# Sums of quarter products kept in a PSUM bank, and a reordered passage between two experts

## The chip, the core and the metric

The kernel runs on one core of a Trainium2 chip. The core has five engines that work side by side and wait for each other by semaphores: TensorE (PE, matrix products, with the load of its stationary operand counted apart as PEld), VectorE (DVE), ScalarE (ACT), GpSimd (POOL) and SyncE (SP, which here starts transfers). Products land in PSUM, whose banks hold 512 float32 values in each of 128 partitions. The metric is the time of one execution on the device, in microseconds (us).

## The reference

A windowed attention is followed by a mixture of experts with one expert per token. Attention works on `q`, `k`, `v` of shape (4, 8, 768, 64); its result is laid out as `x` of shape (3072, 512).

```python
logits = xn @ en.T / tau                   # cosine of token and expert, 8 experts
expert_idx = np.argmax(logits, axis=1)
gate_w = probs[np.arange(N), expert_idx]
for e in range(E):
    mask = expert_idx == e
    h = np.maximum(x[mask] @ w1[e], 0.0)   # 512 -> 1024
    out[mask] = gate_w[mask, None] * (h @ w2[e])   # 1024 -> 512
```

All is float32.

## The kernel before

**Stages.** Attention and routing take the first 190 us or so; the change does not touch them. They end with the first layer (line 670) for a first block of 256 rows of expert 0, whose hidden values are `fhT`. From there the program is straight: the second layer of that block, then the eight experts in turn, each with the rows that are left for it (at most 512).

**Order.** Inside the expert stage the order of instructions on every engine is the order of the program text (`tc.manual_schedule`). Each engine works through its own list in order; an instruction that waits holds all behind it.

**Arms.** The number of rows of an expert is known only when the routing has run. So the first layer and part of the second stand in a `tc.Switch` with one arm for each width. An engine jumps into the arm and, at its end, jumps out to the code behind it. `give_hint` (called in `choose_next`) announces the next jump; `take_width` loads the width of the expert after the next one into a register. In this run the widths are 160, 320, 512, 320, 352, 384, 480 and 384 for experts 0 to 7. TensorE and ScalarE take the switch of expert 0; VectorE joins from expert 1 on.

**First layer.** Expert 0 uses `first_by_eight`, plain products. Experts 1 to 7 use `first_by_seven`: the weights and the tokens are cut into two by two quarters each, and seven products of sums of quarters take the place of eight (a scheme of the Strassen-Winograd kind). Each product fills two banks of the pool `big`, which has four. VectorE adds the product to what was summed so far and writes it to `hT`; ScalarE applies the Relu in place (`bend`). `out` holds the four quarters of the result, q11, q12, q21, q22. `between` puts the transposes of the next expert's rows (`turn_row`, line 1010, copied by ScalarE at line 1013) behind the last products, and `fill` one of four weight sums (`wsum`) for this expert's second layer behind an addition.

**Sums at the arm's end.** At the end of the arm of experts 1 to 6, VectorE makes twelve sums (`making`): four `hsum` of the hidden values (lines 1071 to 1074), four `xsum` of the next expert's tokens (lines 1046 to 1049) and four `fsum` of its first weights (lines 1071 to 1074 again, larger).

**Second layer.** The rows beyond the first 256 (the first 128 in expert 0) are done in the arm, by plain products (`second_in_arm`, line 1206; `part_in_arm`, line 1219). The first 256 rows are done behind the arm by `second_pair`, seven products again, each of four matrix products in one bank of `big` (line 1106); VectorE copies, adds and gates them (lines 1130 to 1117). The first 128 rows of expert 0 go through `second` (line 1024): eight products into one bank of a pool of its own, `work0`, and a gating by VectorE (line 1029). In the trace, a float32 matrix product is two records.

**Passage from expert 0 to 1.** TensorE's list: the seven products of the first block; 16 transposes; the arm of expert 0; the jump out; `second` with its eight products; the arm of expert 1. VectorE makes the weight sums, waits for the row numbers of experts 0 and 1 (line 1620), makes `hsum`, serves the pair, prepares row numbers for all experts, and makes the sums for expert 1.

**GpSimd** gathers rows (line 985) and scatters results (line 1225) in program order; results of one expert are scattered behind the gathers for the expert after the next one.

Of the kernel before, what the change touches and what calls it, by code (L numbers as in the profile page):

```python
# [9 lines left out]
F32 = mybir.dt.float32  # L10
I32 = mybir.dt.int32
AF = mybir.ActivationFunctionType
ALU = mybir.AluOpType
# [7 lines left out]
P = 128  # L21
NEG = 1e9
CAP = 512
PIECES = 32
FIRST = 256
LACE = 16
# [987 lines left out]
             in_=laced(ps[:])[:, a])  # L1014


def second(k, rows, hT, w2, j, pool, later=None, between=None):


    nc = k.nc  # L1020
    mt, ids, _ = rows
    ps = pool.tile([P, k.DM], F32, name="work", tag="work")
    for f in range(k.NF):
        nc.tensor.matmul(ps[:], lhsT=hT[:, f, j * P : (j + 1) * P], rhs=w2[:, f, :],  # L1024
                         start=f == 0, stop=f == k.NF - 1)
        if between and f == 0:
            between()
    y = k.yp.tile([P, k.DM], F32, name="y", tag="y")
    nc.vector.tensor_scalar_mul(y[:], ps[:], mt[:, j, 2:3])

    def scatter():
        scatter_rows(k, y[:], ids[:, j, 1:2])

    if later is None:
        scatter()
    else:
        later.append(scatter)


def right_sums(k, b, t, over=False):  # L1040
# [47 lines left out]
    return left_sums(k, a, k.hsum)  # L1088


def second_pair(k, rows, a, left, w2, sums, later=None, between=None):


    nc, tt = k.nc, k.nc.vector.tensor_tensor
    mt, ids, _ = rows
    b = [[w2[:, 4 * i : 4 * i + 4, j * 256 : (j + 1) * 256] for j in range(2)] for i in range(2)]
    t1, t2, t3, t4 = sums
    s1, s2, s3, s4 = left
    tmp = k.tp.tile([P, 5, 256], F32, name="ptmp", tag="ptmp")
    p1, p4, p5, u2, u4 = (tmp[:, i] for i in range(5))  # L1100
    y = [k.yp.tile([P, k.DM], F32, name="y", tag="y") for _ in range(2)]

    def product(x, w):
        ps = k.big.tile([P, CAP], F32, name="big", tag="big")
        for f in range(4):
            nc.tensor.matmul(ps[:, 0:256], lhsT=x[:, f, :], rhs=w[:, f, :], start=f == 0, stop=f == 3)  # L1106
        return ps[:, 0:256]


    copy = nc.vector.tensor_copy  # L1110

    def add(out, x, z):
        tt(out=out, in0=x, in1=z, op=ALU.add)

    def last(i, j, x, z):

        nc.vector.scalar_tensor_tensor(out=y[i][:, j * 256 : (j + 1) * 256], in0=x, scalar=gate[i], in1=z,  # L1117
                                       op0=ALU.mult, op1=ALU.add)

    def finish(i):  # L1120
        def scatter():
            scatter_rows(k, y[i][:], ids[:, i, 1:2])

        if later is None:
            scatter()
        else:
            later.append(scatter)

    gate = [mt[:, i, 2:3] for i in range(2)]
    copy(out=p1, in_=product(a[0][0], b[0][0]))  # L1130
    if between:
        between()
    add(y[0][:, 0:256], product(a[0][1], b[1][0]), p1)
    copy(out=p4, in_=product(a[1][1], t4))
    copy(out=p5, in_=product(s1, t1))
    nc.scalar.mul(y[0][:, 0:256], y[0][:, 0:256], gate[0])
    add(u2, product(s2, t2), p1)
    add(u4, u2, p5)
    add(p4, u2, p4)
    nc.scalar.mul(p5, u4, gate[1])  # L1140
    nc.scalar.mul(p4, p4, gate[1])
    nc.scalar.mul(u4, u4, gate[0])
    p7 = product(s3, t3)
    last(1, 1, p7, p5)
    last(1, 0, p7, p4)
    finish(1)
    last(0, 1, product(s4, b[1][1]), u4)
    finish(0)

def split_rows(k, mt):
# [100 lines left out]
def first_by_seven(k, now, hT, w, between, spare):  # L1256


    nc, h = k.nc, w // 2
    a = first_weights(k, now.w[0])  # L1260
    b = [[now.xT[:, 2 * i : 2 * i + 2, j] for j in range(2)] for i in range(2)]
    s1, s2, s3, s4 = now.first_sums
    t1, t2, t3, t4 = now.token_sums
    out = [[laced(hT[:, 4 * i : 4 * i + 4, 0:w])[:, j] for j in range(2)] for i in range(2)]
    part = [slice(0, 2), slice(2, 4)]
    number = [0]

    def product(x, y):
        banks = []
        for c in part:  # L1270
            ps = k.big.tile([P, CAP], F32, name="big", tag="big")
            for i, f in enumerate(range(c.start, c.stop)):
                for l in range(2):
                    nc.tensor.matmul(ps[:, i * 256 : i * 256 + h], lhsT=x[:, l, f * P : (f + 1) * P], rhs=y[:, l, 0:h],  # L1274
                                     start=l == 0, stop=l == 1)
            banks.append((c, ps[:].rearrange("p (f n) -> p f n", f=2)[:, :, 0:h].rearrange("p f (q i) -> p f q i", i=LACE)))
        between(number[0])
        number[0] += 1
        return banks

    def add(to, x, z):
        nc.vector.tensor_tensor(out=to, in0=x, in1=z, op=ALU.add)  # L1282

    def fill():
        if spare:
            spare.pop(0)()

    def bend(x):
        nc.scalar.activation(x, x, AF.Relu)  # L1289

    (q11, q12), (q21, q22) = out
    for c, ps in product(a[0][0], b[0][0]):
        nc.scalar.copy(out=q21[:, c], in_=ps)
    for c, ps in product(a[0][1], b[1][0]):
        add(q11[:, c], ps, q21[:, c])
        bend(q11[:, c])
    fill()
    for c, ps in product(s2, t2):
        add(q21[:, c], ps, q21[:, c])
    fill()  # L1300
    for c, ps in product(s1, t1):
        add(q22[:, c], ps, q21[:, c])
    fill()
    for c, ps in product(s4, b[1][1]):
        add(q12[:, c], ps, q22[:, c])
        bend(q12[:, c])
    fill()
    for c, ps in product(s3, t3):
        add(q22[:, c], ps, q22[:, c])
        bend(q22[:, c])  # L1310
        add(q21[:, c], ps, q21[:, c])
    for c, ps in product(a[1][1], t4):
        add(q21[:, c], ps, q21[:, c])
        bend(q21[:, c])


def expert(k, now, coming, widths):


    tc = k.tc  # L1320
    w1, w2 = now.w
    hT = new_hidden(k)
    if coming:
        coming.xT = new_turned(k)

    def between(f):
        for j in {5: (0,), 6: (1, 2), 7: (3,)}.get(f if now.e == 0 else f + 1, ()) if coming else ():
            turn_row(k, coming.rows, coming.xT, j, k.nc.scalar.copy)

    a = [[hT[:, 4 * j : 4 * j + 4, i * P : (i + 1) * P] for j in range(2)] for i in range(2)]  # L1330
    now.sums, spare = weight_sums(k, w2)
    left, making = hidden_sums(k, a)
    if coming:
        coming.token_sums, more = token_sums(k, coming.xT)
        making += more
        if now.e:
            coming.first_sums, more2 = first_sums(k, coming.w[0])
            making += more2
    tiles = range(2 if now.e else 1, CAP // P)
    steps = widths_of(now.e)  # L1340
    for arm in tc.Switch(now.width.index, len(steps), hint=now.width.hint):
        w = steps[arm]
        if now.e:
            first_by_seven(k, now, hT, w, between, list(spare))
            for make in making:
                make()
        else:
            first_by_eight(k, now.xT, w1, hT, w, between)
        for size in (64, 32):
            if w % (2 * size) >= size:  # L1350
                part_in_arm(k, now, hT, w2, w // (2 * size) * 2 * size, size)
        for j in tiles:
            if j < w // P:
                second_in_arm(k, now, hT, w2, j)

    def scatters():
        for j in tiles:
            scatter_rows(k, now.y[:, j - 1, :], now.tile_ids[:, j : j + 1])
        for size in (64, 32):
            scatter_rows(k, now.y_part[size][:], now.parts[size][0], P // size)  # L1360

    def choose_next():
        if coming:
            give_hint(k, coming.e, widths[coming.e])
        if now.e + 2 < k.E:
            widths.append(take_width(k, now.e + 2))

    out = [scatters]
    if now.e:
        second_pair(k, now.rows, a, left, w2, now.sums, out, choose_next)  # L1370
    else:
        second(k, now.rows, hT, w2, 0, k.work0, out, choose_next)
        for make in more:
            make()
    return out


def widths_of(e):
    return WIDTHS[PAIR:] if e else WIDTHS
# [160 lines left out]
def kernel(  # L1540
# [13 lines left out]
    n = Net()  # L1554
    n.tc, n.nc = tc, tc.nc
    nc = n.nc
# [24 lines left out]
    with ExitStack() as moe:  # L1581
# [52 lines left out]
        with tc.manual_schedule(engines=ORDERED | set(ARMS) | {mybir.EngineType.Pool}):  # L1634
# [5 lines left out]
            coming = prepare(0)  # L1640
# [6 lines left out]
            left, making = hidden_sums(n, a)  # L1647
            for make in making:
                make()
            second_pair(n, n.first.rows, a, left, n.w[0][1], sums)  # L1650
            coming.xT = new_turned(n)
            for j in range(CAP // P):
                turn_row(n, coming.rows, coming.xT, j, (nc.scalar.copy, nc.vector.tensor_copy)[j % 2])
# [9 lines left out]
            for e in range(n.E):  # L1663
# [8 lines left out]
                    scatter()  # L1672

                nc.gpsimd.drain()
                pending = expert(n, now, coming, widths)
            for scatter in pending:
                scatter()
    n.scatters = None
# [30 lines left out]
```

## Time and profile before

| what | value |
|---|---|
| time of 3 runs, median (lowest to highest) | 537.62 us (535.7 to 541.6) |
| the profiled execution: its time, its span | 536.57 us, 534.4 us |
| PE busy | 500.3 us, 94% of the span |
| PEld, DVE, ACT, POOL busy | 77%, 62%, 36%, 28% |
| mean granted clock of TensorE | 0.982 |
| products of the first layer, line 1274, chain that ended last | 23% of the span |
| products of the pairs, line 1106, chain that ended last | 17% of the span |

The span runs from the first to the last instruction of one execution; about 2 us of the execution's time lie around it. "Busy" of an engine is the time in which it works on an instruction. "Issue" in a line means that the engine waited for nothing that the profile shows. PEclk is the clock that TensorE was granted, 1.00 being full speed.

### The profile page before, as it was taken

The numbers are of one execution on the slowest core, as the hardware profiler recorded it, in microseconds if no ns is written. First come the engines' busy times: TensorE is split into PE (matmuls) and PEld (weight loads), VectorE is DVE, ScalarE is ACT, GpSimd is POOL, SyncE is SP. The second block draws the span as 40 slices with busy tenths as digits, with TensorE's granted clock in tenths as the row PEclk, the third lists the DMA queues.
The fourth block names the chain that finished last, engine by engine and source line by source line (L and its number), as shares of the span: only waits on it lengthen the run. The fifth ranks groups of instructions, "written<-read, shape, count | busy, mean of one in ns | idle before, by whom it ended". The sixth has DMA issues, their size and how long they took to land.

```text
span 534.4 us, 13806 instructions
## 1 busy us (share of the span) xinstructions
PE 500.3 (94%) x5606; PEld 413.4 (77%) x5606; DVE 329.1 (62%) x664; ACT 193.5 (36%) x491; POOL 151.4 (28%) x169
## 2 busy tenths in 40 slices
PE   7999999999988999779799999979989999999993
PEld 6677787887766889469688579869869789869963
DVE  5656867766776845638737735856745764662832
ACT  4866766767653313213021202312311311412210
POOL 4221121342463434614313022412312140012021
PEclk9999999999999999899999999989989999999997
DMA  9999989999434558652452055526336335001001
GB/s 172 201 186 199 222 218 191 203 225 206 120 91 132 119 143 218 234 190 82 170 197 81 2 200 199 158 95 218 98 137 216 103 141 198 1 25 56 1 20 47
DMA packets 111421, 76.32 MB, mean 143 GB/s; under 512 B 87077, under 2 KB 95269, under 8 KB 111281
## 3 DMA queue, kind: packets, MB, share of 16 engines
q1 hardware_dynamic: 102769, 59.00, 41.7%
q0 software_dynamic: 6912, 15.26, 9.0%
q8 instruction: 63, 1.03, 0.9%
q14 instruction: 77, 0.63, 0.4%
q10 hardware_dynamic: 1600, 0.39, 0.3%
HBM read 61.66 MB, written 17.16 MB: 147 GB/s over the span
## 4 chain that ended last, share of the span: by engine, by line
PE 78%; DVE 7%; issue 5%; ACT 3%; POOL 2%; DMA 2%; SPq 1%; ACTq 0%; DVEq 0%; POOLq 0%
PE big L1274 23%; PE big L1106 17%; PE work L1206 6%; PE od L508 6%; PE pa L479 4%; PE pa L454 3%; PE work L1219 3%; PE od L518 3%; PE work L1010 3%; PE pa L670 2%; ACT ex L485 2%; PE big L1249 2%; PE work L1024 2%; PE pa L581 1%; PE pa L558 1%
## 5 line engine op out<-in xcount | busy, mean ns | idle before, releaser
L1282 DVE TENSOR_TENSOR hT<-big,hT 128x320 f32<-128x320 f32 (+4 forms) x98 | 52.3, 561 | 57.3 <-PE big L1274 40.4
L492 DVE TENSOR_TENSOR ex<-ex,table 126x768 f32<-126x768 f32 x64 | 60.9, 959 | 37.3 <-ACT ex L485 37.0
L1274 PE MATMUL big<-xT,w1t 128*128 128x160 f32 (+4 forms) x336 | 58.3, 330 | 3.5 <-DVE hT L1282 3.5
L1274 PEld LDWEIGHTS big<-xT,w1t 128*128 128x128 f32 x336 | 54.6, 190 | 6.3 <-DVE hT L1282 3.8
L485 ACT ACTIVATE ex<-pa 126x384 f32<-126x384 f32 (+1 forms) x128 | 53.3, 476 | 15.6 <-PE pa L479 14.5
L1106 PE MATMUL big<-wsum,hsum 128*128 128x256 f32 x192 | 48.6, 412 | 7.8 <-DVE ptmp L1130 7.8
L985 POOL DMA_INDIRECT xg<-x_dram,idss x32 | 38.7, 1211 | 60.3 <-PE big L1274 26.3
L1225 POOL DMA_INDIRECT out_dram<-y_arm,tids x17 | 18.8, 1108 | 123.7 <-ACT y_arm L1208 99.1
L1106 PEld LDWEIGHTS big<-wsum,hsum 128*128 128x128 f32 x192 | 39.5, 208 | 15.6 <-DVE ptmp L1130 9.1
L508 PE MATMUL od<-ex,v 126*64 126x192 f32 (+1 forms) x576 | 46.2, 305 | 0.1
L1289 ACT ACTIVATE hT<-hT 128x320 f32<-128x320 f32 (+4 forms) x56 | 27.8, 539 | 36.2 <-DVE hT L1282 36.1
L508 PEld LDWEIGHTS od<-ex,v 126*64 126x64 f32 x576 | 34.6, 136 | 7.9 <-issue 3.5
L1013 ACT COPY xT<-work 128x256 f32<-128x256 f32 x60 | 18.8, 380 | 58.1 <-PE work L1010 57.7
L1274 PE MATMUL big<-xsum,fsum 128*128 128x160 f32 (+4 forms) x224 | 39.6, 330 | 0.0
L256 POOL DMA_INDIRECT meta<-mt,slot x24 | 26.6, 1108 | 39.1 <-DVE xs L590 10.8
L479 PE MATMUL pa<-qT,kT 64*32 64x128 f32 (+3 forms) x2048 | 37.2, 263 | 0.3
L479 PEld LDWEIGHTS pa<-qT,kT 64*32 64x32 f32 (+1 forms) x2048 | 29.1, 105 | 10.6 <-issue 6.1
L1274 PEld LDWEIGHTS big<-xsum,fsum 128*128 128x128 f32 x224 | 36.1, 190 | 1.1
L1206 PE MATMUL work<-w2t,hT 128*128 128x512 f32 x80 | 35.1, 594 | 0.0
L1225 POOL DMA_INDIRECT out_dram<-y,idss x15 | 14.9, 993 | 58.9 <-DVE y L1117 55.2
L429 POOL COPY v<-v 30x896 f32<-30x896 f32 (+1 forms) x15 | 16.7, 1125 | 51.3 <-DMA v<-in_v_dram 16.0
L1206 PEld LDWEIGHTS work<-w2t,hT 128*128 128x128 f32 x80 | 14.9, 190 | 17.4 <-issue 17.2
(242 smaller groups left out, 865.9 us busy)
## 6 DMA issues: line engine op xcount, KB each, us to landing
w1t<-in_moe_w_dram SPq DMA_DIRECT2D x6, 2048.0 KB
w2t<-in_moe_w_dram SPq DMA_DIRECT2D x6, 2048.0 KB, 11.0
v<-in_v_dram SPq DMA_DIRECT2D x32, 192.0 KB, 4.7
x_dram<-xs SPq DMA_DIRECT2D x23, 256.0 KB, 3.8
k<-in_k_dram SPq DMA_DIRECT2D x28, 192.0 KB, 4.8
q<-in_q_dram SPq DMA_DIRECT2D x28, 192.0 KB, 4.7
w1t<-in_moe_w_dram SPq DMA_DIRECT2D x32, 128.0 KB, 5.0
w2t<-in_moe_w_dram SPq DMA_DIRECT2D x32, 128.0 KB, 4.7
```

Source lines behind the costliest of these rows:

```text
L256: i = nc.gpsimd.indirect_dma_start(out=k.meta[:], out_offset=bass.IndirectOffsetOnAxis(ap=slot[:, t : t + 1], axis=0), in_=mt[:, t, :], in ...
L479: i = nc.tensor.matmul(u.sp[e][k0:k1, a * n + c0 : a * n + c1], lhsT=t.kT[rows, j, k0:k1], rhs=t.qT[rows, j * BLK + c0 : j * BLK + c1], st ...
L485: nc.scalar.activation(u.ex[:, e], u.sp[e][0:ROWS, 0 : 2 * u.n].rearrange("p (a c) -> p a c", a=2), AF.Exp, scale=k.scale)
L492: nc.vector.tensor_tensor(out=exv, in0=exv, in1=tab[:, :, 0 : u.n // BLK, :], op=ALU.mult)
L508: nc.tensor.matmul(g.od[a][e * D : (e + 1) * D, at : at + c1 - c0], lhsT=g.v[0:ROWS, 2 * a + e, u.j, :], rhs=u.ex[:, e, a, c0:c1], start=f ...
L985: k.nc.gpsimd.indirect_dma_start(out=xg[:], out_offset=None, in_=k.x_dram[0 : upto or k.N + 1, :], in_offset=bass.IndirectOffsetOnAxis(ap= ...
L1106: nc.tensor.matmul(ps[:, 0:256], lhsT=x[:, f, :], rhs=w[:, f, :], start=f == 0, stop=f == 3)
L1206: nc.tensor.matmul(ps[:], lhsT=hT[:, f, j * P : (j + 1) * P], rhs=w2[:, f, :], start=f == 0, stop=f == k.NF - 1)
L1225: i = k.nc.gpsimd.indirect_dma_start(out=k.out.rearrange("t (i m) -> (t i) m", i=n), out_offset=bass.IndirectOffsetOnAxis(ap=ids, axis=0), ...
L1274: nc.tensor.matmul(ps[:, i * 256 : i * 256 + h], lhsT=x[:, l, f * P : (f + 1) * P], rhs=y[:, l, 0:h], start=l == 0, stop=l == 1)
L1282: nc.vector.tensor_tensor(out=to, in0=x, in1=z, op=ALU.add)
L1289: nc.scalar.activation(x, x, AF.Relu)
```

## The change

Two matrix products whose results are summed can go into the same bank: the second adds to what the first left there. The change uses this in both schemes of seven products. In `first_by_seven` the seven products go into three pairs of banks (x, y, v) rather than seven, and the partial sums are read out between two additions. In `second_pair`, now a generator that the caller steps through, they go into three banks (m, n, v). The order of the products changes: a00·b00, s2·t2, a01·b10, s3·t3, then s1·t1, a11·t4, s4·b11 (the first block of expert 0 has a11·t4 ahead of s1·t1). The quarter of the first layer that is finished last is now q12, where it was q21. Some copies and gatings of the pair move from VectorE to ScalarE, and `choose_next` stands behind the pair's first product and ScalarE's two reads of it.

In the passage from expert 0 to 1, the first block's last two products (s1·t1, s4·b11) move behind expert 0's arm, half of the eight products of `second` moves into the arm, ahead of the jump, and the gating and scattering of both move later. Line numbers shift: 1274 becomes 1265, 1282 becomes 1277, 1106 becomes 1101, 1024 becomes 1020; sums at 1046 to 1049 and 1071 to 1074 are now at 1038 to 1041 and 1063 to 1066; the adds of the pair stand at 1104 and the last steps at 1108.

```diff
-def second(k, rows, hT, w2, j, pool, later=None, between=None):
...
+def second(k, ps, hT, w2, fs):
+    for f in fs:
+        k.nc.tensor.matmul(ps[:], lhsT=hT[:, f, 0:P], rhs=w2[:, f, :], start=f == 0, stop=f == k.NF - 1,
+                           skip_group_check=True)
+
+def end_second(k, rows, ps, later):
     mt, ids, _ = rows
     y = k.yp.tile([P, k.DM], F32, name="y", tag="y")
+    k.nc.vector.tensor_scalar_mul(y[:], ps[:], mt[:, 0, 2:3])
+    later.append(lambda: scatter_rows(k, y[:], ids[:, 0, 1:2]))
...
-def second_pair(k, rows, a, left, w2, sums, later=None, between=None):
+def second_pair(k, rows, a, left, w2, sums, later, split=False):
...
-    copy(out=p1, in_=product(a[0][0], b[0][0]))
-    if between:
-        between()
-    add(y[0][:, 0:256], product(a[0][1], b[1][0]), p1)
-    copy(out=p4, in_=product(a[1][1], t4))
-    copy(out=p5, in_=product(s1, t1))
-    nc.scalar.mul(y[0][:, 0:256], y[0][:, 0:256], gate[0])
-    add(u2, product(s2, t2), p1)
-    add(u4, u2, p5)
-    add(p4, u2, p4)
...
-    p7 = product(s3, t3)
-    last(1, 1, p7, p5)
-    last(1, 0, p7, p4)
-    finish(1)
-    last(0, 1, product(s4, b[1][1]), u4)
-    finish(0)
+    def product(ps, x, w, add=False):
         for f in range(4):
+            nc.tensor.matmul(ps, lhsT=x[:, f, :], rhs=w[:, f, :], start=f == 0 and not add, stop=True, skip_group_check=True)
+
+    def plus(out, x):
+        nc.vector.tensor_tensor(out=out, in0=x, in1=p1, op=ALU.add)
...
+    m, n = bank(), bank()
+    product(m, a[0][0], b[0][0])
+    nc.scalar.copy(out=p1, in_=m)
+    nc.scalar.mul(p1g, m, gate[1])
+    yield
+    product(n, s2, t2)
+    plus(u2, n)
+    product(m, a[0][1], b[1][0], True)
+    nc.scalar.mul(u2g, u2, gate[0])
+    nc.scalar.mul(y[0][:, 0:256], m, gate[0])
+    product(n, s3, t3, True)
+    plus(u3, n)
+    nc.scalar.mul(u3g, u3, gate[1])
+
+    def third():
+        product(n, a[1][1], t4, True)
+        last(1, 0, n, p1g)
+
+    if split:
+        third()
+        yield
+    v = bank()
+    product(v, s1, t1)
+    last(1, 1, v, u3g)
+    if not split:
+        third()
     finish(1)
+    product(v, s4, b[1][1], True)
+    last(0, 1, v, u2g)
     finish(0)
+    yield
...
 # first_by_seven: the seven products (those of before each took two new banks and were read and added once)
+    x, y = banks(), banks()
+    product(x, a[0][0], b[0][0])
+    for ps, q in pairs(x, q21):
+        nc.scalar.copy(out=q, in_=ps)
+    product(y, s2, t2)
+    plus(y, q21, q12)
+    product(x, a[0][1], b[1][0], True)
+    for ps, q in pairs(x, q11):
+        nc.scalar.activation(q, ps, AF.Relu)
+    product(y, s3, t3, True)
+    plus(y, q21, q22)
+    v = banks()
+    product(v, s1, t1)
+    plus(v, q22, q22, True)
+    product(y, a[1][1], t4, True)
+    plus(y, q21, q21, True)
+    product(v, s4, b[1][1], True)
+    plus(v, q12, q12, True)
...
 # expert, at the end of each arm
+        if ps:
+            second(k, ps, hT, w2, range(k.NF // 2))
...
 # expert, behind the switch
     if now.e:
-        second_pair(k, now.rows, a, left, w2, now.sums, out, choose_next)
+        products = second_pair(k, now.rows, a, left, w2, now.sums, out)
+        next(products)
+        choose_next()
+        next(products)
+        while left_over:
+            left_over.pop(0)(out)
     else:
-        second(k, now.rows, hT, w2, 0, k.work0, out, choose_next)
+        choose_next()
         for make in more:
             make()
+        left_over.pop(0)(out)
+        second(k, ps, hT, w2, range(k.NF // 2, k.NF))
+        left_over.append(lambda out: end_second(k, now.rows, ps, out))
```

`plus` in `first_by_seven` does VectorE's two additions of a product, with the Relu of ScalarE behind each where its last argument is `True`, and then pops one of the weight sums. The first call of `second_pair` is stepped twice before the transposes; its rest is what `left_over` holds first.

## The prediction

> **What bounds the kernel now.** I read the page, then TensorE's waits behind the first expert work, then the timelines of PE and DVE around each wait, then the windows for the clock. PE is busy 94% of the span, and its busy time hardly changes, so only its pauses, and the slow clock behind them, can move the time. From 180 us on they are these (engine, line, releaser: total, times, longest):
>
> ```profile
> PE big L1106 <- DVE ptmp L1130: 7.8, 3, 2.8
> PE big L1274 <- DVE hT L1282: 3.5, 1, 3.5
> PE work L1024 <- issue: 3.0, 1, 3.0
> PE big L1249 <- issue: 0.4, 1, 0.4
> ```
>
> The 3.0 follows the jump out of expert 0's arm. The 3.5 is expert 1's fourth product waiting for VectorE. The 7.8 lies in the second layer of experts 1, 3 and 4. PE's timeline shows all three kinds (start, duration, work, idle before):
>
> ```profile
> 221.08 8.83 PE L1024 MATMUL work<-w2t,hT 128*128 128x512 f32 x16 [3.03 <-issue]
> ...
> 239.94 2.44 PE L1274 MATMUL big<-xT,w1t 128*128 128x160 f32 x16 [3.51 <-DVE hT L1282]
> ...
> 264.19 5.41 PE L1106 MATMUL big<-wsum,hsum 128*128 128x256 f32 x16 [2.83 <-DVE ptmp L1130]
> ```
>
> At 264.19 PE had done four products of the pair in four banks; the fifth needs the bank that L1130 reads. VectorE was late: the sums for the next expert stand in its order before the pair, and then comes its own jump out of the arm.
>
> ```profile
> 252.09 0.69 DVE L1072 TENSOR_TENSOR hsum<-hT 128x512 f32<-128x512 f32 x1 [0.75 <-ACT hT L1289]
> ...
> 260.77 1.22 DVE L1074 TENSOR_TENSOR fsum<-w1t,fsum 128x1024 f32<-128x1024 f32 x1
> 263.71 0.42 DVE L1130 COPY ptmp<-big 128x256 f32<-128x256 f32 x1 [1.71 <-issue]
> 264.66 0.43 DVE L1113 TENSOR_TENSOR y<-big,ptmp 128x256 f32<-128x256 f32 x1 [0.53 <-DVE ptmp L1130]
> ```
>
> From L1074's start to L1130's start are 2.94 us here, and 2.80, 4.14 and 2.84 at experts 3, 4 and 5. After such a wait the clock (second last group: PEclk) halves:
>
> ```profile
> 266.00:268.00 2.00, 2.00 (x6) 1.53 (x5) 1.18 (x3) 0.32 (x1) 0.00 (x0) 0.50 0.04 8
> ```
>
> The 24 matmuls behind it took 7.13 us; in expert 2, without a wait, 5.18. So a wait costs about 1.95 more than itself.
>
> **The change, part by part.** One product of a pair is 8 matmul records, 1.73 us (5.18/3).
>
> *Passage from expert 0 to 1, removed.* Four of the eight L1024 products (8 records, 3.43 us at 0.43 each) go ahead of the jump. From the start of L1219 to the end of the stall are 1.95 + 3.03 = 4.98 us; the cover becomes 1.95 + 3.43 = 5.38, so 3.03 goes, and with it the half clock (8.67 us for what takes 6.87: 1.80). VectorE's jump into expert 1's arm took 6.6 us (L1049 at 232.79 to L1282 at 239.39). In the new order 3.43 us of L1024 and three products (6.5) stand between its last work and PE's fourth product: 9.9 against 6.6, so 3.51 goes too. Removed: 8.34. Without that cover, up to 3.0 of the stall stays.
>
> *Passage, added.* The first pair's second product becomes (s2, t2). It needs the third hsum operation, and hsum stands behind the casts of the row numbers:
>
> ```profile
> 193.92 0.17 DVE L1620 CAST idss<-mts 128x8 int32<-128x8 f32 x1 [0.56 <-DMA mts<-meta]
> ...
> 195.91 0.69 DVE L1073 TENSOR_TENSOR hsum<-hsum,fhT 128x512 f32<-128x512 f32 x1
> ```
>
> PE is done with the first product at 190.88 + 1.73 = 192.61 and gets s2 at 196.60 + 0.06: a wait of 4.05 that the old order did not have (its first three products need at most wsum). Half clock behind it: 1.8. The split pair has no other product between n's read and n's third use, nor between v's read and its second: twice 0.08 + 0.42 + 0.06 = 0.55. Added: 4.05 + 1.8 + 1.1 = 6.95. On POOL the first pair's two scatters move behind expert 0's; the gathers they stood before had no waiter. SP's weight load stands behind the same last read of w2, some 2 us later, and is needed 25 us after. Passage: -1.4.
>
> *Second layer of experts 1, 3 and 4.* Three products, not four, run ahead before VectorE is needed: the fourth adds into n, which u2 must have read. Three delays for u2 against the old copy: the quarter finished last is now q12, which all four hsum operations wait for, so L1071 no longer runs ahead (+0.72, the spacing of two such operations); choose_next's register work now stands ahead of VectorE's first read. It took part of the 0.95 from L1130 to L1113; the first pair, without it, has 0.52 there. Ahead of the read it costs 0.43 to 0.95; I take 0.9, because all of it is now serial. So PE resumes 1.62 later, with four products to do, not three (+1.73): +3.35 each, 10.05 for three. The half clock was there before and stays.
>
> *Expert 5* has no wait now: L1130 runs at 433.99, and PE comes to its fourth product at 427.70 + 3 x 1.73 = 432.88. Now u2 runs at 433.99 + 1.62 = 435.61 and PE resumes at 436.09: a wait of 3.2. Four of five such gaps (2.2 to 3.5 us) had half clock behind them, so 0.8 x 1.95 = 1.6 more. Together 4.8; bounds 2.7 (0.43 for the registers, full clock) to 5.2. Experts 2, 6 and 7 have VectorE back before the third product ends: 0.
>
> *ScalarE reads m twice* (0.40 + 0.50) before the third product may add to it. Its jump out of the arm is not seen: L1208 starts at 514.17 in expert 7, and the next operation comes 3.86 later, held by VectorE. Bounds for experts 2, 6 and 7: 0 (jump free) to 1.5 (3.86). I take VectorE's 2.9, the nearest row: 514.17 + 2.9 + 0.9 = 518.0 against 517.4, some 0.7 each, 2.1 in all. In experts 1, 3, 4, 5 VectorE's wait covers it.
>
> *Fewer operations*: VectorE loses 4 adds per arm and 5 operations per pair, ScalarE some bends. I cost this at nothing, because there they wait for PE (L1282 idles 40.4 us for L1274). If PE's cover went, it would be 0.5 us an operation.
>
> Sum: -1.4 + 10.05 + 4.8 + 2.1 = +15.5 on the execution's own 536.57: 552. The median of the runs, 537.62, lies 1 us above that execution; I leave this in the range.
>
> **Two rules weighed.** The trace halved the clock after waits of 2.83, 2.70 and 2.23 us and not after 3.51. The Trainium skill ("TensorE: Matmul & The Clock Gate", "Why this matters for your kernels") puts the limit at idle gaps of about 3 us; by it the old waits would have kept the clock and the new, longer ones would lose it, for 5.9 us more (3 x 1.95), a sum of 558. VectorE's jump cost 2.8 us or more in every arm, near or far. The skill ("Runtime: NRT & Kernel Launch", "Instruction fetch mechanics") has a taken branch stall only where its target lies outside a window of two pages; by it the shorter arms could jump free, which would take some 11 us off the sum (4 x 2.85), to 541.
>
> **Rivals.** (1) *Not slower*: VectorE's jump out becomes free. For: its arms lose 4 operations. Against: expert 5's jump is shorter than expert 1's and cost the same. Then u2 comes 2.85 earlier at four experts (-11.4), expert 5 keeps its clock (-1.6) and ScalarE's 2.1 goes: 552 - 15.1 = 537. It decides from about 2.5 us per jump. (2) *No half clock* behind the long waits: the gap of 3.51 had none. Passage -1.8, expert 5 -1.6, three experts -1.95 each: 552 - 9.3 = 543. (3) *First pair not late*: hsum in time, 552 - 5.9 = 546; against it is the cast at 193.92. (4) *The passage does not do what it says*: the fetch outlasts the moved products and VectorE is late again, 3 to 5 us back: 556.
>
> **Chances.** Forecast 0.55; rival 1 0.12 (a third of it faster); rival 2 0.15; rival 3 0.08; rival 4 0.10. About 1% is what a measurement can tell from no change. Faster by over 1%: 0.04; within 1%: 0.11 (the rest of rival 1, a little of 2 and 3); slower: 0.85. Range: from 541 (rival 2 with ScalarE's term at 0) to 557 (rival 4, or ScalarE's upper bound, 2.4 more, with one half clock more, 1.95).
>
> **What would show it.** After: no wait at L1020 behind expert 0's arm and none in expert 1's first layer; PE idle about 4 us in the first pair before (s2, t2); waits of about 6 us at the fourth product of experts 1, 3, 4 and about 3 at 5, each released by the add of L1104, whose start lies some 15 us behind the arm's last first-layer product; half clock behind them. The forecast is wrong if L1104 starts within 1 us of L1066's end, or if PE runs through the first pair.

## The result and the profile after

The changed kernel took 560.75 us (median of 4 runs, 559.46 to 563.77) against 536.71 for the kernel before on the same chip: a ratio of 1.044, 95% interval 1.036 to 1.052. The forecast was 552.0 with a range of 541 to 557; the sign was right, but the loss was half as large again, 24 us where 15.5 were expected, and the time lies above the range. The profiled execution took 559.46 (536.57 before).

TensorE's waits from 175 us on, the same view of the changed kernel as the prediction showed of the kernel before (engine, tile, line and what released it: total us, times, longest):

```profile
PE big L1101 <- DVE ptmp L1104: 8.8, 5, 3.5
PE work L1211 <- ACT hT L1279: 4.6, 4, 1.2
PE big L1101 <- ACT ptmp L1117: 3.7, 3, 2.3
PE big L1101 <- DVE hsum L1065: 3.6, 1, 3.6
PE big L1101 <- DVE y L1108: 3.0, 1, 3.0
PE work L1198 <- ACT hT L1279: 2.6, 3, 1.3
PE big L1265 <- DVE hT L1277: 1.6, 2, 1.4
PE big L1265 <- issue: 1.6, 1, 1.6
PE big L1101 <- issue: 1.2, 1, 1.2
```

Of the old waits, the 3.5 of expert 1's first layer is gone and the 3.0 behind the jump has become 1.2. The 7.8 in the pairs of experts 1, 3 and 4 has become 12.5 (8.8 + 3.7, with 0.5 of it in the first block). New are 3.6 for the hidden sums, 3.0 for L1108, 7.2 (4.6 + 2.6) for the Relu at L1279, in all seven experts, 1.6 for VectorE in the first layers of experts 3 and 4 (1.37 and 0.25), and 1.6 at the entry of expert 2's arm. Nothing in the prediction speaks of the last three.

TensorE's timeline gives the ledger. Each stretch runs from its first matmul to the first of the next; for an expert it is first layer, arm and pair. The forecast's terms are put where they belong. Below, experts 1, 3, 4 and 5 are called narrow, 2 and 6 wide; expert 7 has the width of 5, but makes no sums for a next expert.

| stretch | before | after | difference | forecast |
|---|---|---|---|---|
| first block to expert 1's first layer | 38.87 | 44.84 | +5.97 | +2.12 |
| expert 1 | 41.41 | 40.82 | -0.59 | -0.16 |
| expert 2 (wide) | 51.74 | 54.20 | +2.46 | +0.7 |
| expert 3 | 37.56 | 42.41 | +4.85 | +3.35 |
| expert 4 | 40.42 | 42.61 | +2.19 | +3.35 |
| expert 5 | 38.90 | 42.85 | +3.95 | +4.8 |
| expert 6 (wide) | 49.07 | 50.69 | +1.62 | +0.7 |
| expert 7 | 37.16 | 37.86 | +0.70 | +0.7 |
| sum | | | +21.15 | +15.56 |

Another 2.4 us lie ahead of the first block (it starts at 193.31, before at 190.88), in stages that the change does not touch. In the twelve experiments below it starts anywhere from 188.94 to 195.93, so I take them for the spread of runs, not for the change. The ledger is that of one execution on each side; the last section shows that the half clock in it differs between executions of the same kernel.

The passage, TensorE first (start, duration, work, idle before it), then VectorE:

```profile
198.83 0.45 PE L1101 MATMUL big<-wsum,hsum 128*128 128x256 f32 x1 [3.63 <-DVE hsum L1065]
...
226.35 1.97 PE L1101 MATMUL big<-wsum,hsum 128*128 128x256 f32 x8 [1.22 <-issue]
231.30 3.58 PE L1101 MATMUL big<-w2t,hsum 128*128 128x256 f32 x8 [2.99 <-DVE y L1108]
```

```profile
226.82 1.25 DVE L1066 TENSOR_TENSOR fsum<-w1t,fsum 128x1024 f32<-128x1024 f32 x1
228.00 0.68 DVE L1038 TENSOR_TENSOR xsum<-xT 128x512 f32<-128x512 f32 x1
...
230.77 0.48 DVE L1108 SCALAR_TENSOR_TENSOR y<-big,emt,ptmp 128x256 f32<-128x256 f32 x1
```

The first of the two products left over ends at about 228.3. The second adds into the same bank, which L1108 must have read, and L1108 stands behind four sums of expert 1's weights and four of its tokens: VectorE works without a pause until 230.77. The eight matmuls behind this wait took 3.58 us, those before it 1.97: the clock was halved.

Expert 1's pair, TensorE, then VectorE, then ScalarE:

```profile
256.38 3.67 PE L1211 MATMUL work<-w2t,hT 128*64 128x256 f32 x32 [1.11 <-ACT hT L1279]
...
270.21 1.99 PE L1101 MATMUL big<-wsum,hsum 128*128 128x256 f32 x8 [3.54 <-DVE ptmp L1104]
```

```profile
265.94 1.23 DVE L1066 TENSOR_TENSOR fsum<-w1t,fsum 128x1024 f32<-128x1024 f32 x1
269.73 0.42 DVE L1104 TENSOR_TENSOR ptmp<-big,ptmp 128x256 f32<-128x256 f32 x1 [2.57 <-issue]
```

```profile
260.18 0.47 ACT L1213 ACTIVATE y<-work,pgate 128x256 f32<-128x256 f32 x1 [3.49 <-issue]
263.88 0.37 ACT L1116 COPY ptmp<-big 128x256 f32<-128x256 f32 x1 [3.22 <-issue]
```

The first product behind the first layer reads the quarter that was bent last, and waits 1.11 for it. From the start of VectorE's last sum in the arm to the start of u2 (L1104) are 3.79 us, where before the first read came after 2.94. ScalarE needs 3.70 from its last operation in the arm to its copy of m.

### The profile page after: what moved, and what is told of

It is laid out like the page before. It is cut to its first block, busy times and chain, and to the rows that moved or that the text cites. A ratio compares the mean times of both kernels' runs of the same rounds, so it can differ in the third digit from the quotient of the medians.

```text
span 557.7 us, 13682 instructions
## 1 busy us (share of the span) xinstructions
PE 504.8 (91%) x5606; PEld 411.3 (74%) x5606; DVE 302.3 (54%) x596; ACT 195.9 (35%) x499; POOL 148.8 (27%) x169
## 5 line engine op out<-in xcount | busy, mean ns | idle before, releaser
L1277 DVE TENSOR_TENSOR hT<-big,hT 128x320 f32<-128x320 f32 (+4 forms) x70 | 39.3, 566 | 75.9 <-PE big L1265 55.7
L1101 PEld LDWEIGHTS big<-wsum,hsum 128*128 128x128 f32 x192 | 37.4, 199 | 24.1 <-DVE ptmp L1104 10.2
L985 POOL DMA_INDIRECT xg<-x_dram,idss x32 | 34.7, 1085 | 57.0 <-PE big L1265 34.3
L1104 DVE TENSOR_TENSOR ptmp<-big,ptmp 128x256 f32<-128x256 f32 x16 | 6.8, 425 | 55.2 <-PE big L1101 46.8
L1101 PE MATMUL big<-w2t,hT 128*128 128x256 f32 x112 | 28.7, 397 | 3.7 <-ACT ptmp L1117 3.7
```

Source lines behind the costliest of these rows:

```text
L985: k.nc.gpsimd.indirect_dma_start(out=xg[:], out_offset=None, in_=k.x_dram[0 : upto or k.N + 1, :], in_offset=bass.IndirectOffsetOnAxis(ap= ...
L1101: nc.tensor.matmul(ps, lhsT=x[:, f, :], rhs=w[:, f, :], start=f == 0 and not add, stop=True, skip_group_check=True)
```

## The experiments

Ratios are to the kernel before on the same chip and in the same batch of runs; its medians there lay between 534.15 and 541.46, so kernels of different batches are compared by ratio.

**The parts by themselves.** Three kernels each do one part of the change and keep the rest of the kernel before.

First layer alone:

```
-    for c, ps in product(s3, t3):  ... (seven products in banks of their own)
+    x, y = banks(), banks()
+    product(x, a[0][0], b[0][0])  ... (as in the change)
```

> Only the first layer's scheme of seven is the new one; pair and passage are those of before. Theory W (the loss is made of waits that the new order brings): the quarter finished last is now q12, the head of hT, so the next product waits 1.1 to 1.3 us for its Relu in experts 2, 5 and 6 and 0.2 in 7 (3.9), and in experts 1, 3 and 4 VectorE comes to the pair 0.7 later each (2.2); expert 1's wait of 3.5 for VectorE stays. Together 6 to 8 us slower than before, about 543, and PE's matmuls as fast as before. Rival A (adding into a bank that was read in between costs TensorE time in every product): PE's busy time grows with the products, in expert 7 as in expert 2, and no new wait is needed. Rival L (jumps only got longer with other code sizes): waits at the entries of arms and behind them, none at the Relu.

It took 540.71 us, ratio 1.006 (1.002 to 1.010), less than expected. TensorE's waits:

```profile
PE big L1106 <- DVE ptmp L1130: 4.9, 4, 1.8
PE work L1219 <- ACT hT L1287: 4.6, 4, 1.2
...
PE work L1206 <- ACT hT L1287: 2.6, 3, 1.3
```

The Relu's 7.2 us stand here without the rest of the change. But the old wait for VectorE fell from 7.8 to 4.9 and nothing behind it ran at half clock: the pairs of experts 1, 3 and 4 took 14.58, 14.52 and 13.51 us instead of 16.97, 16.84 and 16.38. In a narrow expert the new wait mostly takes the place of a later one; in a wide one (2, 6) it is lost.

The pair alone, in the first block and in experts 1 to 7:

```
-        second_pair(k, now.rows, a, left, w2, now.sums, out, choose_next)
+        products = second_pair(k, now.rows, a, left, w2, now.sums, out)   # the new one
+        next(products); choose_next(); next(products)
```

> Only the pair is the new one (in the first block too, not split); first layer and passage are those of before. Theory W: in experts 1, 3 and 4 the fourth product, not the fifth, waits for VectorE, whose read stands behind the register work: 0.9 + 1.7 = 2.6 each; expert 5 gets a wait of 2.5 to 4; the first block waits about 4 for hsum, with up to 1.8 of half clock; experts 2, 6 and 7 lose up to 0.8 each. The two waits of the old passage (3.0 and 3.5) stay. Together 14 to 18 us slower than before, 551 to 555. Rival A: the waits are no longer than before, and each of the seven products is slower. Rival L: the loss lies at the jumps' ends in all experts alike.

It took 553.97 us, ratio 1.027 (1.024 to 1.030), as expected: this is the bulk of the loss.

```profile
PE big L1109 <- ACT ptmp L1125: 9.3, 4, 3.0
PE big L1109 <- DVE ptmp L1112: 6.4, 3, 4.4
...
PE big L1109 <- DVE hsum L1073: 3.3, 1, 3.3
```

Yet the first row is a surprise: ScalarE, not VectorE, is what the third product of experts 1, 3, 4 and 5 waits for first (2.66, 2.73, 0.94 and 2.97 us). The prediction gave ScalarE's late exit to experts 2, 6 and 7. A product by itself keeps its 1.73 us, so adding into a used bank is not slow in itself; only the waits are.

The passage alone, with the old first layer and the old pair in experts 1 to 7:

```
-        products = second_pair(k, now.rows, ...); next(products); choose_next(); next(products)
+        old_pair(k, now.rows, a, left, w2, now.sums, out, choose_next)
```

> Only the passage from expert 0 to 1 is the new one (the first block's pair is new and split); first layer and pair of experts 1 to 7 are those of before. Theory W: the first block waits 3.6 for hsum and 0.5 for u3, the jump leaves 1.2 and VectorE is 3.0 late for the last product with 1.7 of half clock behind it, against 3.0 + 1.8 + 3.5 that go: 2 to 4 us slower than before, about 539.5. Rival P (the passage does what it is for, and the loss lies elsewhere): 3 to 8 us faster than before, about 531. Rival L: as W, and a wait of 1.6 at the entry of expert 2's arm too, 541.

It took 537.96 us, ratio 0.998 (0.995 to 1.001): no difference, where 2 to 4 us more were expected. Waits of 2.59 for the hidden sums and 2.77 for L1108 replace the stall and expert 1's old wait. Together the parts make 0.6 + 2.7 - 0.2 = 3.1%, the whole 4.4% (3.6 to 5.2). The waits of 1.22 behind the jump and of 1.58 at the entry of expert 2's arm show in none of the parts; but neither do they show in the next kernel, the whole change with two products exchanged, which waits 1.24 at the entry of expert 7's arm instead. Whether they make up the rest is not settled, and since the interval of the whole begins at 3.6, a part of the gap may be noise.

**The Relu at the end of the first layer.** In the whole change the last two products are exchanged, so that the last quarter is not the one at the head of the arm's next product:

```
-    product(y, a[1][1], t4, True);     plus(y, q21, q21, True)
     product(v, s4, b[1][1], True);     plus(v, q12, q12, True)
+    product(y, a[1][1], t4, True);     plus(y, q21, q21, True)
```

> The whole change, with the last two products of the first layer in the other order: s4 b11 (q12) before a11 t4 (q21), so that the quarter finished last lies at the end of hT, as before the change. Theory W: the wait at the first product behind the first layer (1.1 to 1.3 us in experts 1 to 6) goes; in experts 2, 6, 7 all of it is gained (2.7), in 1, 3, 4 and 5 only the 0.7 that hsum starts earlier, because VectorE sets the end there (2.9): 5 to 6 us faster than the whole change, about 555. Rival A and rival L: no change from 560.7, within 1 us.

It took 552.00 us, ratio 1.027 (1.023 to 1.032): 1.6% less than the whole change. Both Relu rows are gone from the waits. The stretches of experts 2 and 3 lost 2.5 and 2.6 us, but expert 4 gained 1.8, and the waits for ScalarE in the pairs rose from 3.7 to 8.8.

The same exchange in the first layer alone:

```
 first_by_seven of the exchanged kernel; all else as in the kernel before
```

> The new first layer alone (540.71), with its last two products exchanged as in the run on the whole change. It asks how much of TensorE's 7.2 us of waits for the Relu of the quarter that ends last is a loss by itself. Theory (in the wide experts 2, 6 and 7 nothing else is late, so their 2.7 us are lost; in the narrow experts 1, 3, 4 and 5 TensorE would otherwise wait as much longer for VectorE a few products later, and then with the clock halved): the waits at the first product behind the first layer vanish, the pairs of experts 1, 3 and 4 go back from 14.6, 14.5 and 13.5 to 16 to 17 us, and the time is 537 to 540, that of the kernel before. Rival (all 7.2 us are a loss by themselves): 532 to 534.

540.33 us, ratio 1.000 (0.997 to 1.004). The Relu rows are gone; the wait for VectorE is back at 7.9, and the pairs of experts 1, 3 and 4 at 15.18, 15.17 and 16.57. So most of the 7.2 us, which would be 1.3%, is not a loss by itself: between the two orders lie some 0.6%, with intervals that touch.

**The passage put right.** The first block's products in an order that asks less of VectorE, once with the passage alone and once in the whole change:

```
-    m: a00*b00 | n: s2*t2 | m += a01*b10 | n += s3*t3 | n += a11*t4 || v: s1*t1 | v += s4*b11
+    m: a00*b00 | w: a11*t4 | m += a01*b10 | n: s2*t2 | n += s3*t3 || v: s1*t1 | z: s4*b11
     (each letter a bank; || is expert 0; u4 = u2 + v is one more add on VectorE)
```

> The passage alone (old first layer, old pair for experts 1 to 7), with the first block's seven products in another order: three products that need none of VectorE's sums of hidden quarters first (m, then a11 by t4 in a bank of its own, then m with its second product), then the two in n; and the two products left over behind the jump each in a bank of its own, so that the second no longer waits until VectorE has read the first. Theory (TensorE's waits at these two places are what the passage costs): against the passage alone (537.96) the wait of 2.59 us for the sums falls to under 0.5, the wait of 2.77 us for VectorE behind the jump and the half clock after it (some 1.7 us) go, in all some 6 to 7 us: 531 to 533, under the kernel before (539.22) by 1 to 1.5 per cent. Rival (TensorE only arrives earlier at something else that is late: the copies of the turned rows ahead of expert 0, or the instruction fetch of the jump, which would then show 1 to 3 us more of waiting for nothing the profile names): 536 to 538, not told apart from the passage alone.

534.14 us, ratio 0.996 (0.993 to 1.000); by time alone it is not told apart from the passage alone. The profile shows both waits gone and the stretch from the first block to expert 1 at 37.48 us instead of 43.58, and it shows a bit of the rival: TensorE now comes to expert 0's gathered rows before they are there.

```profile
199.09 1.99 PE L1101 MATMUL big<-wsum,hsum 128*128 128x256 f32 x8 [0.52 <-DVE ptmp L1104]
...
204.24 0.63 PE L1010 MATMUL work<-ident,xg 128*128 128x128 f32 x4 [1.32 <-DMA xg<-x_dram,idss]
```

> The whole change (560.75) with nothing but the first block's products in the corrected order: three products ahead of VectorE's sums, and the two products left over behind the jump each in a bank of its own. It asks how much of the loss of the whole change is the passage, which the prediction put at a gain of 1.4. Theory: the waits of 3.63 and 2.99 us go, with the half clock behind the second (1.7); expert 0's gathered rows are then late by about 1.6 us: 6 us less, 553 to 556, the rest of the loss staying with experts 1 to 7. Rival (the time given back in the passage is lost again in expert 1, whose VectorE then enters its arm late): 559 to 561, and a wait for VectorE of 2 to 4 us in expert 1's first layer.

556.68 us, ratio 1.030 (1.024 to 1.037) against 1.044 (1.036 to 1.052): by the medians some 1.3% of the time, about 7 us, is the passage, where the theory had 5 to 8; the intervals just touch. The profile agrees: both waits are gone, and the stretch from the first block to expert 1 is 39.96 us instead of 44.84. The rival's wait in expert 1's first layer did not come, but expert 1's pair now begins 3.42 late, with half clock behind it, and then waits for nothing; the stretch of expert 1 is 39.19 instead of 40.82.

**Four products ahead.** The exchanged kernel (552.0), with the pair of experts 1 to 7 in another order:

```
-    m: a00*b00 | n: s2*t2 | m += a01*b10 | n += s3*t3 | v: s1*t1 | n += a11*t4 | v += s4*b11
+    m: a00*b00 | n: s2*t2 | v: s1*t1 | w: a11*t4 | m += a01*b10 | n += s3*t3 | v += s4*b11
     (u2 = n + p1, v5 = v + p1, w4 = w + p1 on VectorE; the next expert's registers read after them)
```

> The whole change with the last two products of the first layer exchanged (552.0), and in experts 1 to 7 the pair's products in another order: four products in four banks first (m, n, v and a11 by t4), which need nothing that ScalarE or VectorE makes after leaving the arm except the banks, and only then the three that accumulate. Theory (the narrow experts' pairs are long because VectorE and ScalarE leave the arm 4 to 5.5 us after TensorE's last product there, and only two or three products of 1.73 us are queued ahead of the first one that waits for them): with two more products ahead, expert 1's waits of 2.79 and 1.57 us, expert 3's of 2.77 and 0.75, expert 4's of 0.83 and 4.26 and expert 5's of 2.38 us shrink to about 0.9, 0, 1.6 and 0, and most of the half clock behind them goes: pairs of 12.1 to 13.7 us, and in all some 17 to 20 us less: 532 to 535, faster than before by about 1 per cent. Rival (the pair's end is set by VectorE's and ScalarE's own chain, so that the wait only moves on to the next expert's first products): pairs of 12.5, but waits of 2 to 4 us for banks in the next first layer, 543 to 548.

528.57 us, ratio 0.985 (0.978 to 0.992): 4% less than before the edit, and faster than the kernel before. The only wait that TensorE has left in the experts' pairs (same view, from 235 us on), and its timeline of expert 1's pair:

```profile
PE big L1165 <- DVE ptmp L1168: 3.8, 3, 1.4
```

```profile
257.32 1.99 PE L1165 MATMUL big<-w2t,hT 128*128 128x256 f32 x8
259.15 3.62 PE L1165 MATMUL big<-wsum,hsum 128*128 128x256 f32 x16
262.61 1.89 PE L1165 MATMUL big<-wsum,hT 128*128 128x256 f32 x8
264.33 1.89 PE L1165 MATMUL big<-w2t,hT 128*128 128x256 f32 x8
267.65 1.99 PE L1165 MATMUL big<-wsum,hsum 128*128 128x256 f32 x8 [1.43 <-DVE ptmp L1168]
```

Five products run from 257.32 to 266.2 without a pause. VectorE's read comes at 267.18, 3.26 after its last sum in the arm begins. That is 0.7 sooner than before the edit (3.95), because the edit also moves the register reads behind it, but no sooner than in the kernel before (2.94); what is new is that TensorE has work until then. ScalarE's copy of m still comes 5.66 after its last operation in the arm begins; TensorE does not wait for it. The clock did not halve in any pair (13.89, 12.09, 13.83 and 13.44 us in experts 1 to 4).

**The registers.** The pair alone, with the next expert's registers read behind u2:

```
     product(m, a[0][0], b[0][0]); ...
-    yield            # registers and hint are read here
     product(n, s2, t2); plus(u2, n)
+    yield
```

> The pair alone (553.97) with the registers and the hint for the next expert read after VectorE's u2 instead of before it. The prediction put 0.9 us on each of experts 1, 3, 4 and 5 for this. Theory: VectorE's share of the waits falls by 0.9 us in expert 1 (1.25 to 0.35), by 0.78 in expert 3 and by 0.9 in expert 4 (4.40 to 3.5), nothing in expert 5, where ScalarE is what is late: 2.6 us less, 551.4, with 2 us more or less for each stretch of half clock that comes or goes. Rival (the 0.9 us are not on the path, since the jump itself is what VectorE's start waits for): 554.

551.21 us, ratio 1.027 (1.016 to 1.037), where the pair alone has 1.027 (1.024 to 1.030). The profile's waits for VectorE fell in experts 3 and 4 (0.78 to 0, 4.40 to 3.09) and rose in expert 1 (1.25 to 1.75). For the time this is inconclusive. For the register reads it is not: VectorE's first read in expert 1, first in the pair alone, then here:

```profile
267.71 1.22 DVE L1074 TENSOR_TENSOR fsum<-w1t,fsum 128x1024 f32<-128x1024 f32 x1
271.73 0.42 DVE L1112 TENSOR_TENSOR ptmp<-big,ptmp 128x256 f32<-128x256 f32 x1 [2.80 <-PE big L1109]
```

```profile
264.82 1.23 DVE L1074 TENSOR_TENSOR fsum<-w1t,fsum 128x1024 f32<-128x1024 f32 x1
267.73 0.42 DVE L1112 TENSOR_TENSOR ptmp<-big,ptmp 128x256 f32<-128x256 f32 x1 [1.68 <-issue]
```

The read comes 2.91 after the last sum instead of 4.02; in experts 3, 4 and 5 it is 2.86, 4.50 and 2.99 instead of 3.84, 5.79 and 3.97. So the register reads cost 1.0 to 1.3 us there. How much of that reaches TensorE is not told apart: its third product still waits 2.51, 2.90, 0.98 and 2.43 for ScalarE.

**All of it.** Exchange, four ahead and corrected passage in one kernel:

```
 the exchanged kernel, and
-            products = second_pair(n, n.first.rows, a, left, n.w[0][1], sums, out, True)
+            products = first_pair(...)      # the corrected first block
-        products = second_pair(k, now.rows, a, left, w2, now.sums, out)
+        products = four_pair(...)           # four products ahead
```

> Both of the two before in one: the whole change with the first layer's last two products exchanged, four products ahead in the pairs of experts 1 to 7, and the first block's products in the order of the corrected passage. Theory: the gains add, since they lie in different stages: about 533 less 6 for the passage, 525 to 530, 2 per cent under the kernel before. Rival (half clock and jumps land elsewhere, so that the parts do not add): 531 to 537.

524.92 us, ratio 0.978 (0.971 to 0.985); its runs (523.72 to 525.06) lie wholly under those of four products ahead (528.11 to 529.88) on the same chip. Then once more, in a later batch on the same chip, beside the same kernel with the old first layer put back:

```
-    x, y = banks(), banks() ...             # first_by_seven of the change
+    for c, ps in product(a[0][0], b[0][0]): # first_by_seven of the kernel before
+        nc.scalar.copy(out=q21[:, c], in_=ps) ...
```

> The best so far once more, beside the kernel with the old first layer on the same chip: 523.5 to 527, against the kernel before 0.973 to 0.983, if the gain of 2.24 per cent holds; above 530 if the first runs were lucky in half clock.

> The best so far (first layer with its last two products exchanged, four products ahead in the pairs, corrected passage; 524.92) with the first layer put back to the order of the kernel before, in which VectorE adds and ScalarE bends every quarter by itself and ten operations more are done. Theory (once no wait and no half clock is left in it, the first layer's order is worth only what TensorE waits for, and both orders wait for nothing): the same, 523 to 527, at most a few tenths per cent apart. Rival F (fewer operations in the first layer let VectorE and ScalarE leave the arm earlier, which the pair still waits for in experts 1, 3 and 4 by 1.1 us each): 527 to 531, that is 0.5 to 1 per cent slower. Rival R (the Relu of the quarter that ends last costs in the new order even with the exchange): faster, 520 to 523.

523.77 us (0.979, 0.975 to 0.984) and 523.83 (0.980, 0.975 to 0.985). The gain holds, and the new first layer has no measurable part in it: four adds fewer on VectorE in each arm (10, not 14; the expectation's ten was a miscount) buy nothing, though TensorE still waits 0.8 to 1.4 us for VectorE in the pairs of experts 1, 3 and 4 of both kernels. VectorE has caught up by the end of the first layer in either order: in expert 1 it idles 0.59 or 0.60 for TensorE's product before its last add.

## Why the prediction was wrong in size, and where it was right

*What took the sum out of its range.* The stretches lost 5.6 us more than forecast. The passage alone was 3.85 over. Three waits had no term: the Relu (2.5 in experts 2 and 6, where nothing absorbs it), the 1.58 at the entry of expert 2's arm and the 1.37 for VectorE in expert 3's first layer. Against them the second layers of experts 1, 4 and 5 lost 4.5 less than forecast, mostly because the clock stayed full there. That was luck, as the last section shows; without it the forecast would have missed by more.

*The main mechanism was right.* The pair queues three products, not four, before one that VectorE must release, and VectorE leaves the arm late. The term of 3.35 us each held where the clock behaved alike: from the last first-layer product in the arm to the end of the pair, expert 3 grew by 3.27. Its parts were seen as well: from VectorE's last sum to its first read in the pair are 3.79, 3.82, 4.47 and 4.23 us in experts 1, 3, 4 and 5, before 2.94, 2.80, 4.14 and 2.84, on the mean 0.90 more (forecast 0.9, and the run with the registers later shows what takes it); its last sum begins 0.5 to 0.6 later behind its last add of the first layer (forecast 0.72); and one more product stands behind the wait. The step that failed here is "The half clock was there before and stays". In expert 1 it was gone (1.95 less: +1.6), in expert 4 a part of it (0.84) fell ahead of VectorE's wait and cost nothing (+1.67), and in expert 5, where 1.6 was added for it, it did not come (+3.7 against 4.8). Four products ahead showed the mechanism from the other side: the whole of the loss in the pairs went, and more. Of the signs that were named, the idle of about 4 us in the first pair came (3.63), but not the waits of about 6 at the fourth product: they were 3.54, 3.41 and 0.15 in experts 1, 3 and 4, because TensorE had already waited for the Relu and for ScalarE.

*The passage is the term that failed most*: +5.97 in the stretch against +2.12. The step is "twice 0.08 + 0.42 + 0.06 = 0.55", the price of the split pair's second uses of a bank. It holds for n (0.52). For v it assumed that VectorE is free when v is due, while eight sums stand ahead of that read in its queue: 2.99. The half clock came back behind it (about 1.6). A second step failed with it, "the cover becomes 1.95 + 3.43 = 5.38, so 3.03 goes": it took the 4.98 from the start of the arm's last products to the end of the jump as fixed, and here they were 6.80, so that 1.22 of the stall stayed (none with the exchange or with the passage alone, where 5.42 were enough). Against that the hidden sums were late by 3.63, as forecast (4.05), but no half clock followed (1.8 less). The corrected order took both waits away, and by the medians 1.3% of the time.

*The Relu was not in the sum at all.* The step that failed is the first delay of u2, "the quarter finished last is now q12, which all four hsum operations wait for": it followed VectorE's readers of that quarter and not TensorE's. The arm's first product reads it too, through ScalarE. It cost 7.2 us of waits. In the narrow experts most of it was part of the 3.35 already counted, since VectorE would have been late anyway; in experts 2 and 6 it was a plain 1.26 and 1.24. The exchange gave back 1.6% in the whole change, 1.044 to 1.027, and nothing certain in the first layer alone (1.006 against 1.000, with intervals that touch).

*ScalarE's late exit was put in the wrong experts.* The term of 0.7 each in experts 2, 6 and 7 was taken from VectorE's exit of 2.9 us. Measured from the start of ScalarE's last operation in the arm, its copy of m comes after 1.96, 2.65 and 2.48 us in experts 2, 6 and 7, and TensorE's third product waits for it in none of them. In experts 1, 3 and 4 it comes after 3.70, 3.87 and 5.22, and holds the third product for 0.58, 0.83 and 2.30 before VectorE can hold the fourth; there the prediction had VectorE's wait cover it. The two waits stand in series. That the first mostly shortened the second, and so cost little by itself, is argued and not shown; in expert 4 only 0.15 of the second was left. Why the exit differs is open: in expert 5 it is 2.54 here and 5.53 with the pair alone.

*Costed at nothing, and rightly*: the fewer operations. Old and new first layer in the best kernel are 0.06 us apart, which shows it for VectorE's four adds in each arm; the five operations fewer in each pair were not tested by themselves. ScalarE loses no bends: it does eight in expert 1's first layer before and after.

*The rivals.* The jump out of the arm did not become free: 2.94 us had become 3.79. That also bears on the second rule weighed: by the Trainium skill ("Runtime: NRT & Kernel Launch", "Instruction fetch mechanics") a taken branch stalls where its target lies outside a window of two pages. No exit of VectorE from the narrow arms went without one here: the shortest idle behind its last sum, before and after the change, was 1.58 us. Whether any target lay inside the window, no run shows. The rival without half clock behind the long waits was half right: it stayed away in the first block and in experts 1 and 5, and came in experts 3 and 4 and behind the 2.99 for L1108. The third, hidden sums in time, did not come: they were 3.63 late. The fourth rival, a passage that does not do what it says, came true in part (1.22 of the fetch, 2.99 for VectorE), though for another reason than the one given, and it was priced for the passage only.

*Left open.* When the clock halves; the 2.4 us ahead of the first block; why VectorE came late to expert 3's first layer and TensorE to expert 2's arm; and the 1.3% by which the whole is worse than its parts.

## What to carry to other kernels

An accumulation into a bank that another engine must first read turns a free product into one that waits; put ahead of it as much independent work as the slowest reader needs to get there, its exit from a branch included (here 9.86 us from the start of expert 1's pair to VectorE's read). When the order of a producer changes, list every reader of what now comes last, on every engine, and look up what stands in each reader's queue ahead of it. Fewer operations on an engine that only waits are worth nothing (523.83 and 523.77 us with the old and the new first layer); their order is: with the products in one order the kernel took 1.044 of the time before, in another 0.979.

## What the hardware showed

The clock does not follow the length of one wait alone. In expert 3 the kernel before and the passage alone run the same pair, with the same wait; behind it the clock halved in one and stayed full in the other (0.50 from 355 to 357 us before, 1.00 from 355 to 361 us with the passage alone):

```profile
353.49 5.41 PE L1106 MATMUL big<-wsum,hsum 128*128 128x256 f32 x16 [2.70 <-DVE ptmp L1130]
...
355.31 3.72 PE L1162 MATMUL big<-wsum,hsum 128*128 128x256 f32 x16 [2.69 <-DVE ptmp L1186]
```

The mean granted clock also differs between executions of one kernel, from 0.965 to 0.979 with the pair alone and from 0.977 to 0.986 in the changed kernel. So a stretch of half clock that a profile shows, or does not show, is not yet an effect of the change. In the changed kernel the clock halved behind a wait of 2.99 us and not behind 3.54, and not behind 3.63 (columns: window; PE busy and matmuls; granted clock; DMA share; GB/s):

```profile
231.00:233.00 2.00, 1.70 (x4) 0.53 0.05 12
...
270.00:272.00 2.00, 1.79 (x8) 1.00 0.00 0
```

With four products ahead, a wait of 4.05 in the first block did have half clock behind it (0.50 from 200 to 202 us). Where one wait was split into two, as 1.10 and 1.80 in expert 1 of the first layer alone, the clock stayed full. The limit of about 3 us that the Trainium skill states ("TensorE: Matmul & The Clock Gate", "Why this matters for your kernels") is met by 4.05; 3.54 and 3.63, and 3.51 in the kernel before, lie above it and kept the clock full, and 2.70 lies below it and halved it in the kernel before.
